# Diagonals in two column halves, a first block of its own, re-dealt PSUM banks and earlier transposed loads in a fused forward and backward kernel

## The chip, the cores and the metric

The kernel runs on one core of a Trainium2 chip. A core has a matrix engine (TensorE, PE in the profile, with its weight loads as PEld), a vector engine (VectorE, DVE), a scalar engine (ScalarE, ACT), GpSimd (POOL) and a sync engine (SyncE, SP) that here only issues DMAs. All engines run their own instruction streams in order and meet at semaphores. The metric is the device time of one execution in microseconds; a kernel's time is the median of several executions.

## The reference

The function computes a layer, and then the gradients of all its inputs for a given `grad_out`. S is 2048 rows, D is 1024, F is 3584, all bf16:

```python
xn = layernorm(A_q)
# branch A: short convolution of k, times v, then a long convolution along S by FFT
kv = (sum over t of k shifted by t, times shift_k) * v
y  = irfft(rfft(pad(kv)) * rfft(pad(ssm_k)))[:S] + kv * ssm_D
s  = xn * y
# branch B: gated product of two projections and a third one back
h  = (xn @ w_gate) * (xn @ w_up)
g  = silu(h @ w_down)
out = A_q + s * g
```

The outputs are `out` and the gradients by `A_q` (called dx), k, v, `shift_k`, `ssm_k`, `ssm_D`, `w_gate`, `w_up` and `w_down`. Two of them are sums over S for each channel alone: the gradient of `ssm_D` is the sum of dy times kv, and that of `shift_k` is, for each of four shifts, the sum of dk times the shifted k. The kernel computes such a sum as the diagonal of a 128x128 matrix product.

## The kernel before, in words

The 2048 rows are 16 blocks of 128, the 1024 channels 8 slices of 128, and the 3584 hidden columns 14 slabs of 256. U0 to U12 are SBUF regions of 8 KB a partition that change their use from stage to stage. The stages follow each other on PE:

1. **Layer norm and the first two slabs** (to about 60 us). `layer_norm` (L495 and on) takes the blocks in chunks of 2, 2, 4, 4 and 4 and writes transposed, normalised blocks (PE transposes at L542); `gu_unit` multiplies a chunk with a slab of both projections (L567), copies it to `gut` (ACT, L569), multiplies the two halves on DVE to `hN`, and puts off the transposes of `hN` (`turn`, L581) with `defer`. `flush(age)` raises the age of all that is put off and runs those that have reached it; `gu_unit` calls it after every block. `hN` and `gut` have two buffers each.
2. **The other slabs, with the forward convolution** (to 586 us). `make_pump` runs the convolution's generator alongside: each `yield` gives a weight, meant as the step's DVE time in us, and `pump` advances until the weights done reach the share of the matmul units done.
3. **h @ w_down and the gate** (to 796 us). L964 makes two PSUM banks for a block; `gate` turns them on ACT and DVE into `out` and the gradients that the rest needs, `dbm` among them, and defers its transposes (L1003).
4. **dh and the gradients of w_gate and w_up** (796 to 1451 us). `dh_half` (L1082) and `dw_slab` (L1101) share the PSUM tiles `psb`, which ACT copies out (L1084 to `dht`, L1105 to `wb`); DVE multiplies `dht` into the `U` tiles. The backward convolution runs alongside through `bpump`: first `dy_forward` (per slice: the diagonal product at L803 for the gradient of `ssm_D`, then a forward transform through `psS` and `psP`), then 16 units of `product`, `inv8` and a tail, whose matmuls (L407, L904) write the PSUM tile `psY` that ACT copies out (L882, L906).
5. **The gradient of w_down** (1451 to 1690 us, L1181), into `psb` too. Its outputs leave from U12 by DMAs on SP's queue. SP also issues here the transposing loads of w_gate and w_up (`load_wgu`, L1152) for the next stage.
6. **dx** (1690 us to the end): `dx_part` (L1212) multiplies transposed pieces of the gradient (`dgut`, read by transposing DMAs at L1206 on SP's queue) with those weights, 14 pieces for each group of four blocks; `ln_backward` ends each block. `dk_units` runs alongside, with the diagonal product at L939: for each slice and half, 8 weight loads of 128 columns and 8 matmuls of 512 columns, which are four shifts of 128.

In stages 4 and 5 the eight PSUM banks are dealt out as 4 for `psb`, 1 each for `psS` and `psP`, and 2 for `psY`.

The order of the instructions on each engine is made by a planner: it takes them by priority (the program's order, unless `high_priority` or `issue_after` says otherwise) as their inputs and buffers come free in its own reckoning, so that an engine can be given later work early. On the chip each engine then keeps that order.

Of the kernel before, what the change touches and what calls it, by code (L numbers as in the profile page):

```python
# [19 lines left out]
def build_kernel(  # L20
# [98 lines left out]
    warm = const.tile([P, 1], F32, name="warm")  # L119
    nc.vector.memset(warm[:], 1.0)  # L120
    nc.scalar.activation(warm[:], warm[:], ACT.Sqrt)
    RSTD = const.tile([P, NB], F32, name="RSTD")
    Dbc = const.tile([P, D], BF16, name="Dbc")
    Wbc = const.tile([P, 4, D], BF16, name="Wbc")
# [73 lines left out]
    def tt(o, a, b, op):  # L198
        V.tensor_tensor(o, a, b, op)  # L199
# [101 lines left out]
    def product(A, B, O, wp, conj, src, parts=2):  # L301

        n = 8 // parts
        dst = 1 - src
        for q in range(parts):
            sl = slice(q * n, (q + 1) * n)
            a, b, o = cv(A[:])[:, sl], cv(B[:])[:, sl], cv(O[:])[:, sl]
            m = wp.tile([P, 3, n, 2, 256], BF16, name="m", tag="W")
            m1 = m[:, 0].rearrange("p f k (c d) -> p f k c d", c=2)
            m2 = m[:, 1].rearrange("p f k (c d) -> p f k c d", c=2)  # L310
            n1 = m[:, 2].rearrange("p f k x -> p (f k x)")[:, 0:n * 256].rearrange("p (f k d) -> p f k d", f=n, k=2)
            n2 = m[:, 2].rearrange("p f k x -> p (f k x)")[:, n * 256:].rearrange("p (f k d) -> p f k d", f=n, k=2)
            fk = "p f k c d -> p (f k) c d"
            tt(m1.rearrange(fk), a.rearrange(fk), b.rearrange(fk)[:, :, 0:1, :].to_broadcast([P, 2 * n, 2, P]), MUL)
            for k in range(2):
                tt(m2[:, :, k], a[:, :, k], b[:, :, 1 - k, 0:1, :].to_broadcast([P, n, 2, P]), MUL)
            yield 2.8
            b1, asrc = b[:, :, :, 1, :], a[:, :, :, src, :]
            tt(n1, asrc, b1, MUL)
            tt(n2, asrc, b1[:, :, ::-1], MUL)  # L320
            tt(m1[:, :, :, dst], m1[:, :, :, dst], n1, ADD)
            tt(m2[:, :, :, dst], m2[:, :, :, dst], n2, ADD)
            yield 2.8
            tt(o[:, :, 0], m1[:, :, 0], m1[:, :, 1], ADD if conj else SUB)
            if conj:
                tt(o[:, :, 1], m2[:, :, 1], m2[:, :, 0], SUB)
            else:
                tt(o[:, :, 1], m2[:, :, 0], m2[:, :, 1], ADD)
            yield 1.4
    PROD_W = 14.0  # L330

    def turned(X, to, frm, sign):
# [226 lines left out]
    def gu_unit(sl, b0, n, w, tick):  # L559

        gut = fg.tile([P, 4, 2, SLW], BF16, name="gut")
        hN = fg.tile([P, 4, SLW], BF16, name="hN")
        for i in range(n):
            q, qi = divmod(b0 + i, 4)
            ps = ps_gu.tile([P, 512], F32, name="psg")
            for dc in range(DC):
                gu_mm[0] = nc.tensor.matmul(ps[:], XNT[q][:, dc, qi * P:(qi + 1) * P],  # L567
                                            w[:, dc].rearrange("p a f -> p (a f)"), start=(dc == 0), stop=(dc == DC - 1))
            nc.scalar.copy(out=gut[:, i].rearrange("p a f -> p (a f)"), in_=ps[:])  # L569
            flush(2)  # L570
            tick()
        sta(GUd[sl, b0 // 8][:, b0 % 8:b0 % 8 + n], gut[:, 0:n])
        tt(hN[:, 0:n], gut[:, 0:n, 0], gut[:, 0:n, 1], MUL)
        st(Hd[sl][:, b0:b0 + n, :], hN[:, 0:n])

        def turn():
            hT = fg.tile([P, 2, 4, P], BF16, name="hT")
            ps = ps_tr.tile([P, 2, 4, P], BF16, name="tr")
            for a in range(2):
                for i in range(n):  # L580
                    nc.tensor.transpose(ps[:, a, i, :], hN[:, i, a * P:(a + 1) * P], ident[:])  # L581
            nc.scalar.copy(out=hT[:, :, 0:n], in_=ps[:, :, 0:n])
            fr, so = sl % 12 * SLW, b0 % 8 * P
            st(HTd[b0 // 8][sl // 12][fr:fr + SLW, so:so + n * P].rearrange("(a f) s -> f a s", f=P),
               hT[:, :, 0:n].rearrange("f a i s -> f a (i s)"))
        defer(turn)

    def conv_forward():
# [90 lines left out]
        for ds in range(8):  # L679
# [7 lines left out]

    F_TOTAL = 4 * 20.0 + 8 * (0.2 + FWD4_W + FWD2_W + 1.4 + 1.2 + PROD_W + INV_W + 1.6)
    nop = lambda: None
    slabs = [load_slab(0, nc.scalar)[0]]  # L690
    chunks = [(0, 2), (2, 2), (4, 4), (8, 4), (12, 4)]
    xs = [(b0, n, u8((4, 6, 7)[b0 // 4 - 1], a=4) if n == 4 else lnp.tile([P, n, D], BF16, name=f"x{b0}")[:])
          for (b0, n) in chunks]
    for c in xs[:2]:
        ln_load(*c)
    slabs.append(load_slab(1, nc.sync)[0])
    for c in xs[2:]:
        ln_load(*c)

    def copy_k(dp):  # L700
# [8 lines left out]
    for i, (b0, n, x4) in enumerate(xs):  # L709
# [2 lines left out]
                last, root, xst = layer_norm(*xs[i + 1])  # L712
        for sl in range(2):
            gu_unit(sl, b0, n, slabs[sl], nop)
            if i in (2, 3):
                with tc.issue_after(gu_mm[0].ins):
                    for j in ((3, 4), (2,), (1,), (0,))[2 * (i - 2) + sl]:
                        bcast(j)
        if i == len(xs) - 1:
            with tc.issue_after(root.ins):  # L720
# [67 lines left out]
    def dy_forward(cx, cs):  # L788
# [7 lines left out]
        for ds in range(8):  # L796
# [3 lines left out]
            X = cs.tile([P, 16, 256], BF16, name="DX")  # L800
            ps = ps_y.tile([P, 4, P], F32, name="psY")
            for b in range(NB):
                nc.tensor.matmul(ps[:, 0, :], x[:, b, :], kv[:, b, :], start=(b == 0), stop=(b == NB - 1))  # L803
            yield 0.1
            dt_ = cs.tile([P, P], F32, name="dt_")
            tt(dt_[:], ps[:, 0, :], ident_f[:], MUL)
            dr_ = cs.tile([P, 1], F32, name="dr_")
            V.tensor_reduce(dr_[:], dt_[:], AX.X, ADD)
            V.tensor_copy(ddo[:, ds:ds + 1], dr_[:])
# [5 lines left out]
    def conv_backward():  # L815
        cx = pool("d_cx", 2)
        cs = pool("d_cs", 1)
        yield from dy_forward(cx, cs)
        cs.release()
        cx.release()  # L820
        tfp.release()
# [55 lines left out]
    def dkv_tail(ds, G, tiles, ew):  # L877
        dy, v, ksh = tiles
        y = ew.tile([P, NB, P], BF16, name="yl")
        for rp in range(4):  # L880
            ps = inv8_rows(G, ps_y, rp)
            nc.scalar.copy(out=by_res(y[:], rp), in_=rowps(ps))  # L882
            yield 0.1
        tt(dy[:], dy[:], Dbc[:, ds * P:(ds + 1) * P].unsqueeze(1).to_broadcast([P, NB, P]), MUL)
# [10 lines left out]
    def dh_tail(ds, G, ew):  # L895
        hr = ew.tile([P, 2, 8, P], BF16, name="yl")
        ho = ew.tile([P, 2, P, 8], BF16, name="ho")
        for c in range(2):
            for rq in range(2):
                ps = ps_y.tile([P, 4, P], F32, name="psY")  # L900
                for i in range(4):
                    r = 4 * rq + i
                    for k in range(2):
# [8 lines left out]
    def dk_units(ew, psp):  # L912
# [11 lines left out]
        for i in range(16):  # L924
# [9 lines left out]
                yield 1  # L934
            st(o_dk[:, c, :, dsl], acc[:])
            if c == 0:
                ps = psp.tile([P, 4, P], F32, name="psdk")
            for r in range(8):
                nc.tensor.matmul(ps[:].rearrange("p a b -> p (a b)"), dk[:, r, :],  # L939
                                 kh[:, r:r + 4, :].rearrange("p a b -> p (a b)"),  # L940
                                 start=(c == 0 and r == 0), stop=(c == 1 and r == 7))
            yield 1
            if i < 15:
                kh, dk = load(i + 1)
            if c == 1:
                dt_ = ew.tile([P, 4, P], F32, name="dt2")
                tt(dt_[:], ps[:], ident_f[:].unsqueeze(1).to_broadcast([P, 4, P]), MUL)
                dr_ = ew.tile([P, 4], F32, name="dr2")
                V.tensor_reduce(dr_[:], dt_[:], AX.X, ADD)
                V.tensor_copy(dsko[:, ds, ::-1], dr_[:])  # L950
# [105 lines left out]
    XN = [u8(q, a=4) for q in (7, 8, 9, 10)]  # L1056
    bg = pool("bg", 2, side="right")
    U.append(bg.tile([P, 4096], BF16, name="U12", bufs=1))
    ps_b = ps_tr = pool("ps_b", 4, space=PSUM)
    tr_name[0] = "psb"  # L1060
    ps_c3 = pool("ps_c3", 1, space=PSUM)
    ps_y = pool("ps_y3", 2, space=PSUM)
    bcnt = [0]
    BT = NSL * (8 + 16) + 84.0

# [48 lines left out]
        ld(h, Hd[sl])  # L1114
        return h

    flush()
    for k in (1, 2):
        gu_in(k)
    wdts = [wdt, load_wdt(1)]  # L1120
# [3 lines left out]
        gu_in(k)  # L1124
    first = dh_half(0, wdt)
    DBM = [u8(q, a=4) for q in (0, 1, 4, 5)]
    HSL = (3, 11, 6, 2)
    for sl in range(NSL):
        dgus = [first, dh_half(2 * sl + 1, wdts[sl])]
        if sl + 2 < NSL:  # L1130
# [10 lines left out]
        for k in (2 * sl + 5, 2 * sl + 6):  # L1141
            gu_in(k)

    pieces = [(a, j) for j in range(7) for a in range(2)]
# [2 lines left out]
    def load_wgu(n, store):  # L1149
        a, j = pieces[n]  # L1150
        WGU[n] = store
        nc.sync.dma_start_transpose(out=store, in_=(B_w_gate, B_w_up)[a][:, j * 512:(j + 1) * 512])  # L1152

    flush()
    for k in range(NSL):
        if 0 < k and k + 1 < NSL:
            hs[k + 1] = load_h(k + 1, HSL[(k + 1) % 4])
        if k == 0:
            hs[2] = load_h(2, HSL[2])
        if k in (1, 3, 5, 7):  # L1160
            load_wgu(k // 2, u8(7 + k // 2, a=4))
        if k == 11:

            bdrain()
# [1 line left out]
            gw = pool("gw", 1)  # L1166
            gd = pool("gd", 1)
            for i in range(2):
                load_wgu(4 + i, gw.tile([P, 4, D], BF16, name=f"W{i}")[:])
            load_wgu(6, u8(6, a=4))  # L1170
        if k == 12:
            load_wgu(7, u8(2, a=4))
        if k == 13:
            load_wgu(8, u8(3, a=4))
        h = hs.pop(k)
        for f in range(2):
            wbs = U[12][:].rearrange("p (i d) -> p i d", i=4)[:, (2 * k + f) % 4]
            for dh in range(2):
                ps = ps_b.tile([P, 512], F32, name="psb")
                for b in range(NB):  # L1180
# [3 lines left out]
                btick(2)  # L1184
            f0 = k * SLW + f * P
            ld(o_dwd[f0:f0 + P, :], wbs)
    for p_ in (ps_y, ps_c3, ps_b, bg, bw):
        p_.release()

    gd2 = pool("gd2", 1, side="right")
    gl = pool("gl", 2, side="right")
    gs = pool("gs", 4, side="right")
    kw_ = pool("kw", 1)
# [1 line left out]
    ps_k = pool("ps_k", 1, space=PSUM)  # L1198
    kpump, kdrain = make_pump(dk_units(kw_, ps_k), DK_TOTAL)
    kcnt = [0]  # L1200

    def load_dgut(g, n):

        a, j = pieces[n]
        t = (gd, gd2)[n // 7].tile([P, 4, 512], BF16, name=f"dgut{n}")
        nc.sync.dma_start_transpose(out=t[:], in_=DGd[j, a, 512 * g:512 * g + 512, :])  # L1206
        return t

    def dx_part(t, i, ps, n, dhs=(0, 1)):
        for f in range(4):  # L1210
# [34 lines left out]
            V.scalar_tensor_tensor(dx_t[:, cl], dxn[:, cl], RSTD[:, b:b + 1], dout_t[:, cl], op0=MUL, op1=ADD)  # L1245
            (st if parts == 1 else ld)(o_dx[:, c, r, cl], dx_t[:, cl])

    ts = [load_dgut(0, n) for n in range(7)]
    for i, j in enumerate((11, 0, 1, 4, 5)):
        load_wgu(9 + i, u8(j, a=4))  # L1250
        ts.append(load_dgut(0, 7 + i))
    ts += [load_dgut(0, n) for n in (12, 13)]
    for g in range(4):
        for b in (4 * g, 4 * g + 2):
            if b == NB - 2:
# [86 lines left out]
```

## Time and profile before

| | us |
|---|---|
| time, median of 4 runs (2087.7 to 2102.53) | 2095.59 |
| time of the profiled execution | 2091.74 |
| its span, first to last instruction | 2089.9 |
| PE busy | 2005.5 (96%) |
| DVE busy | 1461.2 (70%) |
| ACT busy | 626.6 (30%) |
| granted TensorE clock, mean | 0.99 |

A row of the waits reads: engine, tile and line of the instruction that waited, then what released it, and then the total in us, the number of waits and the longest. A row of the stretches reads: from and to, length, and the busy time of each engine with its number of instructions, the granted clock, the mean share of the DMA engines and GB/s. A row of the timeline reads: start, duration, engine, line, operation, tiles, number, and in brackets the idle time before it and what ended that.

### The profile page before, as it was taken

What the parts mean: (1) busy time and instruction counts of PE and PEld (TensorE: products, weight loads), DVE (VectorE), ACT (ScalarE), POOL (GpSimd) and SP (SyncE); (2) the same over time, 40 slices, a digit from 0 to 9 for tenths busy, and PEclk for the clock granted to TensorE, in tenths of its full rate; (3) what the DMA queues carried; (4) which work ended last, traced back from release to release, by engine and by line L of the source; (5) the groups of instructions that cost most, each with busy time, mean ns of one, the idle gap of its engine ahead of it and who ended that gap; (6) DMA issues with size and microseconds to landing.
All of it is one profiled execution on the core that took longest, in us unless ns stands there. A gap on an engine that the chain in (4) does not pass through costs nothing.

```text
span 2089.9 us, 28857 instructions
## 1 busy us (share of the span) xinstructions
PE 2005.5 (96%) x11438; PEld 1089.2 (52%) x11626; DVE 1461.2 (70%) x1937; ACT 626.6 (30%) x969; POOL 340.5 (16%) x496
## 2 busy tenths in 40 slices
PE   7989999999999998999899999999999989999998
PEld 3455555555544446666566555564444434444443
DVE  7689898878725555787799999899596024344443
ACT  5734444444423333222222222222122101111112
POOL 3322222121112121000112112111111000110100
PEclk9999999999999999999999999999999999999999
DMA  8776677566598878666889978767964989393921
GB/s 291 239 254 207 219 234 251 185 215 241 174 313 266 258 239 311 217 210 155 264 250 266 228 229 276 217 222 219 228 220 137 230 196 226 94 210 92 222 72 58
DMA packets 454279, 451.29 MB, mean 216 GB/s; under 512 B 236944, under 2 KB 380600, under 8 KB 439680
## 3 DMA queue, kind: packets, MB, share of 16 engines
q1 hardware_dynamic: 308096, 185.89, 34.6%
q0 software_dynamic: 45120, 189.08, 26.9%
q10 hardware_dynamic: 100928, 74.47, 11.6%
q8 instruction: 91, 1.49, 0.3%
q14 instruction: 44, 0.36, 0.1%
HBM read 208.15 MB, written 194.02 MB: 192 GB/s over the span
## 4 chain that ended last, share of the span: by engine, by line
PE 42%; DVE 6%; issue 6%; SPq 4%; DMA 3%; POOL 1%; ACT 0%; another core or an unknown queue 0%; ACTq 0%; DVEq 0%; POOLq 0%
PE psx L1212 17%; PE psb L1101 11%; PE psb L1181 7%; PE psb L1082 4%; SPq L1152 3%; DVE W L199 2%; DVE m L199 1%; PE psdk L939 1%; DVE U L199 1%; DMA dyl<-DYd 1%; DMA B<-HFd 1%; PE psY L904 0%; PE psY L407 0%; SPq L1206 0%; DMA U<-GUd 0%
## 5 line engine op out<-in xcount | busy, mean ns | idle before, releaser
L1101 PE MATMUL psb<-U,U 128*128 128x512 bf16 x1746 | 402.2, 384 | 10.5 <-ACT dht L1084 4.7
L567 PE MATMUL psg<-wslab,U 128*128 128x512 bf16 x1729 | 403.3, 381 | 4.2 <-ACT gut L569 0.7
L1212 PE MATMUL psx<-U,dgut 128*128 128x512 bf16 x1508 | 336.3, 380 | 7.1 <-DMA dgut<-DGd 5.4
L1212 PEld LDWEIGHTS <-dgut 128*128 128x128 bf16 x1792 | 175.6, 98 | 219.0 <-DMA dgut<-DGd 6.9
L1101 PEld LDWEIGHTS <-U 128*128 128x128 bf16 x1792 | 176.9, 99 | 212.3 <-issue 19.3
L567 PEld LDWEIGHTS <-U 128*128 128x128 bf16 x1792 | 173.6, 98 | 187.9 <-issue 5.5
L1082 PE MATMUL psb<-wdt,U 128*128 128x256 bf16 x1792 | 205.9, 275 | 0.0
L569 ACT CAST gut<-psg 128x512 bf16<-128x512 f32 x224 | 131.1, 586 | 219.5 <-PE psg L567 216.7
L1181 PE MATMUL psb<-U,U 128*128 128x512 bf16 x875 | 195.8, 380 | 1.1
L1082 PEld LDWEIGHTS <-U 128*128 128x128 bf16 x1792 | 176.5, 99 | 23.2
L964 PE MATMUL psbm<-U,ht 128*128 128x512 bf16 x766 | 170.4, 379 | 1.2 <-DMA ht<-HTd 0.3
L1105 ACT CAST wb<-psb 128x512 bf16<-128x512 f32 x112 | 65.7, 586 | 320.4 <-PE psb L1101 252.2
L199 DVE TENSOR_TENSOR W<-W 128x1024 f32<-128x1024 f32 (+1 forms) x144 | 149.7, 1058 | 2.7
L199 DVE TENSOR_TENSOR m<-A,B 128x1024 bf16<-128x1024 bf16 (+1 forms) x160 | 116.7, 792 | 40.5 <-issue 22.3
L1181 PEld LDWEIGHTS <-U 128*128 128x128 bf16 x896 | 87.4, 98 | 102.7 <-issue 1.3
L1235 ACT ACTIVATE dx_t<-dxn 128x1024 bf16<-128x1024 f32 (+1 forms) x17 | 17.1, 1007 | 361.8 <-DVE dxn L199 309.8
L199 DVE TENSOR_TENSOR dka<-dkh,Wbc 128x1024 bf16<-128x1024 bf16 x16 | 11.1, 692 | 160.4 <-DMA dkh<-DKSHd 160.4
L964 PEld LDWEIGHTS <-ht 128*128 128x128 bf16 x784 | 76.0, 98 | 89.5 <-DMA ht<-HTd 0.8
L1084 ACT CAST dht<-psb 128x512 bf16<-128x512 f32 x112 | 65.1, 588 | 149.2 <-PE psb L1082 99.3
L1183 ACT CAST U<-psb 128x512 bf16<-128x512 f32 x56 | 32.8, 587 | 164.2 <-PE psb L1181 126.2
L199 DVE TENSOR_TENSOR U<-U,dht 128x2048 bf16<-128x2048 bf16 x56 | 68.1, 1220 | 19.0 <-ACT dht L1084 19.0
L199 DVE TENSOR_TENSOR gg<-bm,sig 128x1024 bf16<-128x1024 bf16 x16 | 11.1, 692 | 91.9 <-ACT sig L982 91.9
(239 smaller groups left out, 2471.4 us busy)
## 6 DMA issues: line engine op xcount, KB each, us to landing
U<-GUd SPq DMA_DIRECT2D x28, 1024.0 KB, 7.0
DGd<-U ACTq DMA_DIRECT2D x56, 512.0 KB, 5.7
GUd<-gut ACTq DMA_DIRECT2D x54, 512.0 KB, 4.5
A<-DYFd POOLq DMA_DIRECT2D x16, 1024.0 KB, 6.4
U<-Hd SPq DMA_DIRECT2D x15, 1024.0 KB, 6.7
out_dram<-wb ACTq DMA_DIRECT2D x224, 64.0 KB, 3.2
Hd<-hN POOLq DMA_DIRECT2D x54, 256.0 KB, 4.6
HTd<-hT POOLq DMA_DIRECT2D x54, 256.0 KB, 4.1
```

The costliest lines, as they stand in the source:

```text
L199: V.tensor_tensor(o, a, b, op)
L567: gu_mm[0] = nc.tensor.matmul(ps[:], XNT[q][:, dc, qi * P:(qi + 1) * P], w[:, dc].rearrange("p a f -> p (a f)"), start=(dc == 0), stop=(dc ...
L569: nc.scalar.copy(out=gut[:, i].rearrange("p a f -> p (a f)"), in_=ps[:])
L964: nc.tensor.matmul(ps[:, dh * 512:(dh + 1) * 512], ht(fc)[:, i * P:(i + 1) * P], WD[fc // 4][:, fc % 4, dh * 512:(dh + 1) * 512], start=(f ...
L1082: nc.tensor.matmul(ps[:, x * SLW:(x + 1) * SLW], DBMT[2 * hf + g][:, dc, (b % 4) * P:(b % 4 + 1) * P], wdt[:, dc, :], start=(dc == 0), sto ...
L1084: nc.scalar.copy(out=dht[:, 2 * e:2 * e + 2].rearrange("p b f -> p (b f)"), in_=ps[:])
L1101: nc.tensor.matmul(ps[:], XN[b // 4][:, b % 4, dc * P:(dc + 1) * P], dgus[b // 8][:, b % 8].rearrange("p a f -> p (a f)"), start=(b == 0), ...
L1105: nc.scalar.copy(out=wb[:].rearrange("p a f -> p (a f)"), in_=ps[:])
L1152: nc.sync.dma_start_transpose(out=store, in_=(B_w_gate, B_w_up)[a][:, j * 512:(j + 1) * 512])
L1181: nc.tensor.matmul(ps[:], h[:, b, f * P:(f + 1) * P], DBM[b // 4][:, b % 4, dh * 512:(dh + 1) * 512], start=(b == 0), stop=(b == NB - 1))
L1183: nc.scalar.copy(out=wbs[:, dh * 512:(dh + 1) * 512], in_=ps[:])
L1212: nc.tensor.matmul(ps[:, dh * 512:(dh + 1) * 512], t[n][:, f, i * P:(i + 1) * P], WGU[n][:, f, dh * 512:(dh + 1) * 512], start=(n == 0 and ...
```

## The change

- **Diagonals.** The product at L803 is made as two products of 64x64, one for each half of the channels, which write the partitions 0 to 63 and 64 to 127 of one PSUM tile; that at L939 as two of 64 x (4 x 64). The mask is a new 128x64 constant `diag`, both halves of the identity in one. DVE's masked multiply and sum take half the columns.
- **First chunk.** The chunks are 1, 1, 2, 4, 4, 4 blocks. The load of the first block comes ahead of slab 0, which moves from ACT's queue to SP's. The places where the broadcast rows are made move on by one chunk.
- **Pace.** The weights that `product` yields become 5.6, 5.6 and 2.8 divided by the number of parts.
- **`flush(3)`** instead of `flush(2)` in `gu_unit`. At the end of stage 3, what is put off gets age -2 instead of being run at once.
- **PSUM.** `psb` gets 3 banks, `psS` and `psP` 2 each, `psY` 1; when `dy_forward` is through, the four of `psS` and `psP` become four `psY` tiles for the tails.
- **Stage 5.** Its outputs leave from a pool `wo` of four tiles, h has three homes instead of four, w_gate and w_up pieces are loaded at steps 1, 2, 3, 4, 5 (before: 1, 3, 5, 7), and the `dgut` pieces of group 0 at steps 6 to 9, 11, 12 and 13 and after; before, all of them after the loop.

```diff
+    diag = const.tile([P, 64], F32, name="diag")
+    nc.vector.tensor_tensor(diag[:], ident_f[:, 0:64], ident_f[:, 64:128], ADD)
...
-            yield 2.8
+            yield 5.6 / parts
...
-            yield 1.4
+            yield 2.8 / parts
...
-            flush(2)
+            flush(3)
...
-    slabs = [load_slab(0, nc.scalar)[0]]
-    chunks = [(0, 2), (2, 2), (4, 4), (8, 4), (12, 4)]
+    chunks = [(0, 1), (1, 1), (2, 2), (4, 4), (8, 4), (12, 4)]
...
-    for c in xs[:2]:
+    ln_load(*xs[0])
+    slabs = [load_slab(0, nc.sync)[0]]
+    for c in xs[1:3]:
...
-                nc.tensor.matmul(ps[:, 0, :], x[:, b, :], kv[:, b, :], start=(b == 0), stop=(b == NB - 1))
+                for j in (slice(0, 64), slice(64, 128)):
+                    nc.tensor.matmul(ps[j, 0, 0:64], x[:, b, j], kv[:, b, j], start=(b == 0), stop=(b == NB - 1))
...
         yield from dy_forward(cx, cs)
+        ps_c3.release()
+        ps_y4.append(pool("ps_y4", 4, space=PSUM))
...
-                nc.tensor.matmul(ps[:].rearrange("p a b -> p (a b)"), dk[:, r, :],
-                                 kh[:, r:r + 4, :].rearrange("p a b -> p (a b)"),
-                                 start=(c == 0 and r == 0), stop=(c == 1 and r == 7))
+                for j in (slice(0, 64), slice(64, 128)):
+                    nc.tensor.matmul(ps[j], dk[:, r, j], kh[:, r:r + 4, j],
+                                     start=(c == 0 and r == 0), stop=(c == 1 and r == 7))
...
-    ps_b = ps_tr = pool("ps_b", 4, space=PSUM)
+    ps_b = ps_tr = pool("ps_b", 3, space=PSUM)
...
-    ps_c3 = pool("ps_c3", 1, space=PSUM)
-    ps_y = pool("ps_y3", 2, space=PSUM)
+    ps_y = pool("ps_y3", 1, space=PSUM)
+    ps_c3 = pool("ps_c3", 2, space=PSUM)
...
-    flush()
+    for e in later:
+        e[0] = -2
...
-        if k in (1, 3, 5, 7):
-            load_wgu(k // 2, u8(7 + k // 2, a=4))
+        if k in (1, 2, 3, 4, 5):
+            load_wgu(k - 1, u8((7, 8, 9, 10, 2)[k - 1], a=4))
+        if k in (6, 7, 8, 9):
+            ts.append(load_dgut(0, k - 6))
...
-    ts = [load_dgut(0, n) for n in range(7)]
     for i, j in enumerate((11, 0, 1, 4, 5)):
         load_wgu(9 + i, u8(j, a=4))
-        ts.append(load_dgut(0, 7 + i))
-    ts += [load_dgut(0, n) for n in (12, 13)]
+        ts.append(load_dgut(0, 9 + i))
```

## The prediction, made before the result was known

> **What bounds the kernel now.** I read the page's busy times first, then the stretches of each stage, then what PE waited for.
>
> ```profile
> PE 2005.5 (96%) x11438; PEld 1089.2 (52%) x11626; DVE 1461.2 (70%) x1937; ACT 626.6 (30%) x969; POOL 340.5 (16%) x496
> ...
> 796.00:1000.00 204.00, 202.76 (x1374) 130.54 (x1389) 156.44 (x236) 58.78 (x103) 14.35 (x27) 0.99 0.71 213
> 1000.00:1451.00 451.00, 431.47 (x2652) 260.30 (x2683) 422.28 (x488) 111.47 (x198) 83.38 (x114) 0.98 0.80 242
> ...
> 1706.00:2081.00 375.00, 372.94 (x1701) 169.66 (x1734) 155.17 (x200) 54.54 (x79) 36.58 (x58) 1.00 0.60 140
> ```
>
> PE is the bound: it idles 84 us of 2090, and in the stretches where the diagonals lie (796 to 1000, 1706 to 2081) it idles 1.2 and 2.1 us. What PE saves or spends there counts in full. From 1000 to 1451 DVE is busy 94% too, so there PE's waits are DVE's lateness, handed on by ACT. PE's own waits are the rest that can be won:
>
> ```profile
> PE tr L542 <- DVE x L539: 11.0, 1, 11.0
> PE tr L581 <- DVE hN L199: 8.9, 10, 2.6
> PE psb L1003 <- DVE dbm L199: 6.7, 1, 6.7
> PE psx L1212 <- DMA dgut<-DGd: 5.4, 3, 3.1
> PE psb L1101 <- ACT dht L1084: 4.7, 2, 4.4
> PE psY L407 <- ACT yl L882: 4.4, 2, 3.8
> ...
> PE psY L904 <- ACT yl L906: 2.8, 1, 2.8
> PE psY L407 <- DVE B L242: 2.8, 1, 2.8
> ```
>
> Nearly every wait in this list is addressed by an edit, so I price the edits against it.
>
> **Pace weights: 0.** `product` has two parts by default and both callers leave it so: 5.6/2 and 2.8/2 are the old 2.8 and 1.4. This edit does nothing.
>
> **`flush(3)`: -6.6 us.** It puts the transposes of `hN` one block, 8 matmuls (8 x 0.216 = 1.7 us), later. Of the 8.9 us of waits, one of 1.4 us at 585.8 is the last unit, which the final `flush()` still runs at once; the longest, 2.6, leaves 0.8; the rest fits into 1.7. 8.9 - 1.4 - 0.8 = 6.7, say 6.6. The ACT copy and POOL store of `hT` come 1.7 us later; their readers are a stage away. Range -4 to -7.
>
> **Age -2 at the end of stage 3: -5.5 us.** PE now starts `dh_half(0)`, which needs only the first eight blocks, and the transposes follow after its four `psb` (7 us). The wait of 6.7 us goes. What comes late next: ACT's copy of the last `psbm` (1.0 us, ended 1.2 us after PE's last matmul), which I take as the new first wait if the first `psb` lies in its banks. DVE's gate ends at 797.1; the `dht` copies have two buffers and its first multiplication is then due, so little queues behind. Range -3 to -6.7.
>
> **First chunk: -1.5 us.** PE begins at 11.0 because DVE does two blocks first, from 5.5. One block saves two statistics pairs and scalings, about 1.6 us of the 5.5, and its 256 KB, alone in front, may land in 3.1 to 4.9 us (the rows of such loads) after its issue at 0.74 where the first data came at 5.5. Against this: slab 0 leaves ACT's queue for SP's and is issued about 0.5 us later (0.45 us an issue), so the later loads, slab 1 among them, stand behind two more issues; a chunk more costs DVE another chain of small operations, about 2 us from 8.3 to 10.5; and units of one block reuse two `gut` buffers after 1.7 us of work where the store lands after 4.5 to 5.8 us. Range -3.5 to +2.
>
> **Gradient pieces: -5.4 us.** Rows of the profile's transposing loads:
>
> ```profile
> L1206 SPq DMA_TRANSPOSE dgut<-DGd x56: 1809/2302/6182, 1631.4 to 1980.7; - x56
> L1152 SPq DMA_TRANSPOSE U<-in_B_w_gate_dram x6: 4419/5676/24397, 1449.1 to 1689.1; - x6
> ```
>
> From 1610 to 1708 SP issues ten weight and fourteen gradient loads, 90 us of issuing in 98 us, and PE meets three pieces not yet there. One weight load (5.7) and four pieces (4 x 2.3) leave this stretch for earlier steps, where SP mostly waits for ACT: it ends some 15 us sooner, the waits go. The nine pieces pass the remaining outputs, h and the row loads in SP's queue; an output held up by 2.3 us leaves from four tiles, used again 28 us later, so it is covered. Not covered is a burst: at 1473 one weight load held SP for 24.4 us, ACT waited 18.1 us for outputs, and PE 2.8. A fifth weight load sits near that place. h with three homes is still loaded a step ahead. Range -6 to +3.
>
> **PSUM: +3.9 us.** A trace row shows the case where `psb` counts:
>
> ```profile
> 1153.23 0.59 ACT L1084 CAST dht<-psb 128x512 bf16<-128x512 f32 x1 [10.15 <-DVE U L199]
> ```
>
> ACT waits for DVE with four `psb` full, PE stops for 4.4 us. I compared each `psb` group's first weight load with the end of ACT's copy three groups earlier. With three banks seven places run short: at 1027 by 0.6, 1120 by 0.7, 1147 by 6.4 (1.75 more than now), 1198 by 3.9, 1293 by 2.3 (0.5 of it there now), 1347 by 0.4, 1380 by 1.85. The one at 1198 takes the place of the 3.8 us that PE waits for `yl` at 1207, in the same ACT stall: net 0.1. Sum 0.6 + 0.7 + 1.75 + 0.1 + 1.8 + 0.4 + 1.85 = 7.2. Four `psY` remove the other `yl` waits, 0.6 and 2.8: +3.8 to 3.9. The waits for `B` stay, they are DVE's. Two banks each for `psS` and `psP`: 0, since PE hardly idles there. Range -3 (if the spare `psY` let PE run ahead in every stall) to +12.
>
> **Diagonals: -6 us.** The rows of before are these:
>
> ```profile
> L803 PEld LDWEIGHTS <-dyx x128: 97/98/98, 814.8 to 973.4; 128*128 128x128 bf16 x128
> L803 PE MATMUL psY<-kvx,dyx x128: 219/219/219, 814.9 to 973.5; 128*128 128x128 bf16 x128
> ...
> L939 PE MATMUL psdk<-kh,dkh x124: 379/379/379, 1658.4 to 2023.4; 128*128 128x512 bf16 x124
> ...
> 1730.13 1.73 PE psdk L939 x8
> ```
>
> Eight dk matmuls take 1.73 us, 0.216 each, 16 times: 27.7 us. If the two column halves run side by side a pair takes as long as one matmul of 256, 0.109 (L1082 makes sixteen in 1.75): 14.0 us, so -13.8. If they run one after the other, 2 x 0.109: +0.3. The dy product is 16 matmuls in about 0.9 us (0.056 each), 8 times: 7.2 us. Halves of 64 columns have little to win there: side by side 0, with each half taking the time of a whole one +7.2.
>
> [...] I take dk at -9 and dy at +3, near the middle, as neither end has a row behind it. Range -14 to +15. DVE's halved mask work is not on PE's path at either place.
>
> **Sum.** -6.6 - 5.5 - 1.5 - 5.4 + 3.9 - 6 = -21.1. The profiled execution, 2091.7 (span 2089.9 and 1.8 around it), becomes 2070.6. It ran 3.9 under the median, so the same step from the median 2095.6 gives **2074.5**. The last 9 us, after PE's last matmul, are unchanged. The likeliest case's own range is 2060 to 2085. About 0.5% (10.5 us: under 2085.1 or over 2106.1) is what a measurement can tell from no change.
>
> **Rivals.**
>
> [...]
>
> *PSUM and SP's queue take back more.* Three `psb` cost 11 with no gain from `psY`, and the burst of weight loads eats 3.4 of the 5.4. -6.6 - 5.5 - 1.5 - 2 + 11 - 6 = -10.6, **2085**. For it: 94% DVE from 1000 to 1451, four stalls of ACT of 4 to 10 us. Against: most stalls are shorter than three groups (5.2 to 10.4 us).
>
> [...]
>
> **Chances.** Main case 0.58, nearly all of it faster; no overlap 0.18 (0.03 faster, 0.11 same, 0.04 slower); banks and queue 0.14 (0.06, 0.06, 0.02); exposed loads 0.10 (slower by 0.09). Faster 0.66, same 0.19, slower 0.15. The range reaches from the main case with every part at a good value (-40: start 3.5, `hN` 7, turn 6.7, pieces 6, diagonals 14, PSUM 3) to just past the second case: **2055 to 2100**, which leaves out the exposed loads and half of what is over 2096.
>
> **What would show it.** `hN` waits of PE near 1 to 2 us; no `dbm` wait at 796; no `dgut` waits after 1690; PE's first matmul before 10 us; `psdk` groups of 1.2 us or less where 1.73 stood, and `psY` groups at L803 of 0.9 to 1.6; waits of `psb` on ACT risen from 4.7 to about 12 and those of `yl` gone. I am wrong if the `psdk` groups stay at 1.7 or grow, if ACT's stalls stop PE for over 15 us, or if outputs held up behind SP's transposing loads stop ACT in stage 5.

## The result and the profile after

The changed kernel takes 2084.37 us (median of 44 runs, 2073.82 to 2100.82); the kernel before took 2093.81 (63 runs). The ratio of the two, each time taken beside the other's, is 0.9963, with a 95% interval of 0.9950 to 0.9976: 7.8 us less (5 to 10.5). 2074.5 and 21 us less were predicted, so the sign was right, the time lies in the stated range, and the gain is little more than a third of the forecast.

The profiled execution was one of the quicker ones (2079.1 us, span 2077.3). Its busy times, stretches cut at its own stage borders, and PE's waits:

```profile
PE 1986.1 (96%) x11691; PEld 1086.4 (52%) x11882; DVE 1450.9 (70%) x1949; ACT 625.1 (30%) x972; POOL 342.4 (16%) x501
...
794.00:1000.00 206.00, 196.44 (x1480) 125.40 (x1493) 156.44 (x239) 60.20 (x104) 15.64 (x28) 0.99 0.77 221
1000.00:1458.00 458.00, 434.35 (x2679) 263.55 (x2709) 423.16 (x492) 112.55 (x199) 83.78 (x114) 0.98 0.77 240
...
1706.00:2068.00 362.00, 356.65 (x1783) 165.62 (x1816) 149.26 (x197) 54.53 (x79) 35.36 (x56) 1.00 0.63 142
```

```profile
PE tr L583 <- DVE hN L201: 10.6, 6, 8.5
PE psb L1089 <- ACT dht L1091: 9.1, 2, 6.0
PE tr L544 <- DVE x L541: 8.0, 1, 8.0
PE psY L420 <- DVE HX L201: 5.9, 4, 2.1
PE psY L807 <- DMA kvx<-KVd: 4.6, 1, 4.6
PE psg L569 <- ACT U L545: 4.5, 2, 3.5
PE psY L409 <- DVE B L244: 4.5, 1, 4.5
...
PE psb L1108 <- ACT dht L1091: 2.9, 2, 1.6
```

PE is busy 19 us less, and it still idles 91 us of the span. The list has no `dbm` of 6.7 us, no `dgut` and no `yl` any more, as foretold; but `hN` stands at 10.6 where it was to fall to 1 to 2, and waits for `kvx` and for ACT's `U` are new. The `dht` row of 9.1 is not: 6.0 of it stand at 1157.8, in the stall that cost 4.4 at 1153.9 before, and 3.1 at 1297.6, near another place that the prediction named. The stretch from 794 to 1000 went from 1.2 us of idle PE to 9.6.

Where the time went is seen best between fixed points of PE's program, which have the same work between them in both kernels but for the diagonals and a few matmuls at two of the borders (starts of weight loads: the one after the n-th of the projections, the first of each stage; dw is the gradients of w_gate and w_up; us):

| stretch | before | after | difference | predicted |
|---|---|---|---|---|
| start to 320th load of the projections | 104.6 | 109.3 | +4.7 | -1.5 |
| 320th to 1280th load | 324.4 | 319.1 | -5.3 | |
| 1280th load to stage 3 | 157.2 | 163.8 | +6.6 | with the line above -6.6 |
| stage 3 to the first dw load | 236.2 | 236.5 | +0.3 | -5.5 |
| first dw load to stage 5 | 628.9 | 629.4 | +0.5 | about +10 (`psb` +7.2, `yl` -0.6, dy +3) |
| stage 5 (to the first load of dx) | 207.8 | 203.3 | -4.5 | -2.8 (`yl`) |
| dx, first to last load | 421.1 | 406.0 | -15.1 | -14.4 |
| last load to the end | 9.7 | 10.1 | +0.4 | 0 |

The sum is -12.4, the span's -12.6 within the rounding. Stage 5 and dx earn more than all of it. The gains on `hN`, at the start and at the end of stage 3 are absent or have turned round: 13.6 us were forecast for the three, and 6.3 were lost.

### The profile page after: what moved, and what is told of

Same layout as the page of the kernel before. It is cut to its first block, busy times and chain, and to the rows that moved or that the text cites. A ratio compares the mean times of both kernels' runs of the same rounds, so it can differ in the third digit from the quotient of the medians.

```text
span 2077.3 us, 29391 instructions
## 1 busy us (share of the span) xinstructions
PE 1986.1 (96%) x11691; PEld 1086.4 (52%) x11882; DVE 1450.9 (70%) x1949; ACT 625.1 (30%) x972; POOL 342.4 (16%) x501
## 4 chain that ended last, share of the span: by engine, by line
PE 51%; issue 23%; DVE 15%; POOL 4%; DMA 4%; ACT 1%; ACTq 0%; POOLq 0%; SPq 0%; DVEq 0%
PE psx L1229 18%; PE psb L1108 10%; PE psb L1206 9%; PE psg L569 5%; PE psb L1089 4%; DVE m L201 4%; DVE W L201 3%; DVE HX L201 2%; DVE U L201 2%; DVE KX L201 1%; DMA dyl<-DYd 1%; PE psP L218 1%; PE psdk L946 1%; PE psS L218 1%; POOL HTd L65 1%
## 5 line engine op out<-in xcount | busy, mean ns | idle before, releaser
L1108 PE MATMUL psb<-U,U 128*128 128x512 bf16 x1746 | 397.3, 382 | 8.6 <-ACT dht L1091 2.9
L1108 PEld LDWEIGHTS <-U 128*128 128x128 bf16 x1792 | 176.0, 98 | 210.6 <-issue 12.2
L1089 PE MATMUL psb<-wdt,U 128*128 128x256 bf16 x1792 | 206.0, 275 | 10.3 <-ACT dht L1091 9.1
L1206 PE MATMUL psb<-U,U 128*128 128x512 bf16 x875 | 194.7, 379 | 1.1
L201 DVE TENSOR_TENSOR W<-W 128x1024 f32<-128x1024 f32 (+1 forms) x144 | 142.7, 1009 | 2.7
L1208 ACT CAST wbs<-psb 128x512 bf16<-128x512 f32 x56 | 32.8, 585 | 159.6 <-PE psb L1206 135.5
```

Source lines behind the costliest of these rows:

```text
L1089: nc.tensor.matmul(ps[:, x * SLW:(x + 1) * SLW], DBMT[2 * hf + g][:, dc, (b % 4) * P:(b % 4 + 1) * P], wdt[:, dc, :], start=(dc == 0), sto ...
L1108: nc.tensor.matmul(ps[:], XN[b // 4][:, b % 4, dc * P:(dc + 1) * P], dgus[b // 8][:, b % 8].rearrange("p a f -> p (a f)"), start=(b == 0), ...
L1206: nc.tensor.matmul(ps[:], h[:, b, f * P:(f + 1) * P], DBM[b // 4][:, b % 4, dh * 512:(dh + 1) * 512], start=(b == 0), stop=(b == NB - 1))
L1208: nc.scalar.copy(out=wbs[:, dh * 512:(dh + 1) * 512], in_=ps[:])
```

## The experiments

The number after "Measured" is the ratio to the kernel before, which ran beside each; the changed kernel's is 0.9963. The median of the kernel before was 2094.3 us beside the first four, 2089.2 beside the next four and 2097.4 beside the last three, so medians in us should not be compared from one of these groups to another. Single executions of one kernel scatter by 12 to 30 us, so the intervals are 5 to 8 us to either side, and where an effect is smaller the stretches of the profiled executions are read instead. Where nothing moved, most of these repeat within 3 us from kernel to kernel; the one from the first dw load to stage 5 lies between 624.9 and 629.4 in the ten kernels that have neither late loads nor a later pump there. Stage 5 and a place near 1010 us scatter more, and are taken up below.

**The diagonals alone**, in the kernel before: the edits at L803 and L939 and the constant `diag`.

> The kernel before with the two diagonals in column halves (and the mask `diag`) and nothing else. Theory 1, the halves run side by side and each edit's gain can be lost again only next to where it is made: PE's groups go from 1.73 to about 1.1 us (dk, 16 times) and from 0.9 to 0.7 (dy, 8 times), the time falls by 11 to 12 us, the stretch from the first to the last matmul of dx shortens by about 10. Theory 2, the planner's new order decides and an edit's place says little: the groups shorten likewise, but the time falls by less than 6 us or rises, with new waits far from the diagonals.

Measured: 0.9952 (0.9923 to 0.9982), 10 us less, with an interval that holds both -4 and -16. The groups settle it. These are pieces of the chain of waits, first of this kernel, then, for the dy product, of the changed one:

```profile
1744.86 2.38 PE psx L1215 x11
1747.24 0.99 PE psdk L943 x16
1748.23 3.35 PE psx L1215 x15
```

```profile
839.98 2.75 PE psb L1108 x12
842.74 0.62 PE psY L807 x32
843.36 0.33 PE psS L218 x2
```

Sixteen matmuls of 256 columns start to start in 0.99 us where eight of 512 took 1.73; within a group the two halves start 2 to 4 ns apart and the next pair 0.109 us later, the turn of one matmul of 256: the halves run side by side. At either end of a group a tenth is lost: the matmul ahead of it keeps the group waiting for 0.309 where 0.216 is its turn, and the last pair takes 0.205 for 0.109. With both ends a dk group costs 1.73 - 0.99 - 0.09 = 0.64 us less, 16 times 10.2 us; a dy group 0.89 - 0.63 - 0.09 = 0.17, 8 times 1.4. Together 11.6 us, as theory 1 has it for the groups. Its other sign, dx shorter by 10 us, did not show in this profiled execution (a span of 2104.2): dx took 423.2 us for 421.1, as PE waited 8.0 for `dgut` and 4.3 for `dxn`, and stage 5 took 11.4 longer, which comes under the paced loads. In the changed kernel, where the `dgut` waits are gone too, dx is 15 us shorter.

**The old start** in the changed kernel: chunks 2, 2, 4, 4, 4 and slab 0 on ACT's queue.

```diff
-    chunks = [(0, 1), (1, 1), (2, 2), (4, 4), (8, 4), (12, 4)]
+    slabs = [load_slab(0, nc.scalar)[0]]
+    chunks = [(0, 2), (2, 2), (4, 4), (8, 4), (12, 4)]
...
```

> The changed kernel with the chunks 2, 2, 4, 4, 4 and slab 0 on ACT's queue, as before. Theory 1, a first block of its own costs time, because ACT's copy of its transposes stands behind the next block's root and because units of one block wait for the stores of `gut`: the 320th weight load of the projections comes at about 105 us again instead of 109.3, and the time is 4 to 5 us under the changed kernel's. Theory 2, the late 320th load comes from the later transposes (`flush(3)`) or from DMA order: it stays at 108 or later and the time is the same within 2 us.

Measured: the 320th load came at 104.2 us, 5.1 sooner than in the changed kernel, as theory 1 has it, though PE there begins at 11.0 instead of 8.0. The 320th load came at 104 to 105 us in all seven kernels with the old chunks, and at 109 in the six others. The time as a whole, 0.9967 (0.9945 to 0.9990), doesn't show it; the profiled execution has an unrelated wait of 5 us for h in stage 5. The changed kernel's timeline shows the first reason, ACT's order:

```profile
11.39 0.20 ACT L520 ACTIVATE r__233<-vpe 128x1 f32<-128x1 bf16 x1 [5.14 <-DVE vpe L518]
11.50 0.99 ACT L545 COPY U<-tr 128x1024 bf16<-128x1024 bf16 x1
```

The transposes of block 0 are ready at 9.1. But the planner put the root of block 1 ahead of their copy on ACT, and that root waits for DVE, which does block 1's statistics and, between them, the new `diag` (1.3 us at 9.54). PE waits 3.5 us; later ACT waits twice 3.3 us for `gut` tiles still being stored, and PE 1.0 and 2.1 for ACT. How the loss divides between these was not tried.

**The gate's last transposes at once**, as before, in the changed kernel.

```diff
-    for e in later:
-        e[0] = -2
+    flush()
```

> The changed kernel with the last transposes of the gate run at once at the end of stage 3, as before. Theory 1, the wait saved there comes back as PE's wait for `kvx` and `dyx`, since the chain from the gate to the first dy product is as long as before: the wait for `dbm` of about 6.7 us returns, the 4.6 us wait for `kvx` goes, and the time is the changed kernel's within 2 us. Theory 2, the wait for `kvx` has another cause (the new PSUM deal, POOL's queue): it stays and the time is 6 to 7 us over the changed kernel's.

Measured: 0.9952 (0.9926 to 0.9978), the profile 2076.9 beside the changed kernel's 2077.3. Of PE's waits

```profile
PE psb L1089 <- ACT dht L1091: 9.5, 2, 6.4
PE tr L544 <- DVE x L541: 7.8, 1, 7.8
PE psb L1009 <- DVE dbm L201: 6.7, 1, 6.7
```

the 6.7 us are back, and the wait for `kvx` is gone. From stage 3 to the first dw load it takes 235.3 us, with the edit 236.5. Theory 1: the edit is worth nothing. The first dy product needs the last block's `dy` written to memory and read back (gate, `DYd`, `dyx`), and the load of `kvx`, which itself needs nothing of the gate, stands behind that of `dyx` on POOL's queue. From the last matmul of stage 3 to the landing of `kvx` it takes 21.3 us before, 22.4 in the changed kernel and 21.6 here, whatever PE does meanwhile. Issuing `kvx` ahead of `dyx` was not tried; `dyx` landed 1.5 us sooner than `kvx`, and it is needed too.

The trace shows too what the wait of 6.7 us costs beside its length. After it, stretches of the kernel before read

```profile
796.00:800.00 4.00, 4.00 (x24) 3.08 (x25) 1.15 (x2) 1.01 (x1) 1.19 (x3) 0.50 1.02 420
804.00:812.00 8.00, 8.00 (x76) 7.18 (x74) 3.19 (x3) 2.67 (x5) 1.05 (x2) 1.00 1.02 402
```

The granted clock is 0.50 in the first, and dh's matmuls start 0.213 us apart there where 0.109 is their turn. So without the wait PE comes to the dy product 18.1 us after the last weight load of stage 3 where it took 26.3: 8.2 us sooner, 5.5 of them the wait. All of it is lost again: 4.6 us in the wait for `kvx`, 3.0 at `psS` and `psP` for ACT and DVE, which the pause seems to have held up too, and about 1 in slow matmuls after that wait (a clock of 0.57 from 816.4 to 820).

**The old PSUM deal** in the changed kernel (`psb` 4, `psS` and `psP` 1, `psY` 2, no `ps_y4`).

> The changed kernel with the PSUM banks dealt as before: 4 for `psb`, 1 each for `psS` and `psP`, 2 for `psY` to the end. Theory 1, three `psb` lengthen what PE loses when ACT waits for DVE: PE's waits of `psb` on ACT fall from 12 to about 5 us, those of `psY` on `yl` return with 3 to 7 us, and the time is 2 to 6 us under the changed kernel's. Theory 2, the spare `psY` are worth more than the bank of `psb`: the time is 2 us or more above it.

Measured: 0.9962 (0.9934 to 0.9990); from the first dw load to stage 5 627.0 us, with the new deal 629.4. PE's waits of `psb` on ACT are 5.2 where they were 12.0, those on `yl` 4.4 where there were none: both as theory 1 says, but they nearly cancel, and 2.4 us is within what this stretch scatters between kernels with the new deal (624.9 to 629.4). From stage 3's first load to stage 5 it is 865.2 us for 865.7. The deal is worth nothing that can be measured here, and neither theory's time came.

**`flush(2)`** in the changed kernel.

> The changed kernel with `flush(2)` in `gu_unit`, as before. Theory 1, putting the transposes off made the planner set DVE's first product of the gate (`so`, which waits for a load) ahead of the last `hN`: with `flush(2)` the order is `hN`, `so` again, the wait of 8.5 us at the end of stage 2 falls to about 1.4, the stretch from the 1280th weight load of the projections to stage 3 to 157 us from 163.8; and the waits for `hN` during the convolution come back with about 5 us between the 320th and the 640th load (110 to 111 us for 105), so that the time is within 2 us of the changed kernel's. Theory 2, the 8.5 us come from elsewhere: they stay, and the time is 5 us above.

Measured: 0.9968 (0.9941 to 0.9996). From the 1280th load to stage 3 157.2 us for 163.8, from the 320th to the 640th 110.8 for 105.0: theory 1 in both halves. Putting the transposes off wins 5.3 us between the 320th and the 1280th load, where DVE is late with `hN` (over all the profiled kernels 319.1 to 322.0 us with `flush(3)`, 323.6 to 324.4 with `flush(2)`), and 6.6 are lost at the end, where the last `flush()` runs the transposes at once in either kernel. That loss is one swap in DVE's order, in the changed kernel (first ACT's copy that makes the last `gut`):

```profile
583.02 0.59 ACT L571 CAST gut<-psg 128x512 bf16<-128x512 f32 x1 [0.67 <-PE psg L569]
...
590.13 0.69 DVE L201 TENSOR_TENSOR so<-xn_t,yf_t 128x1024 bf16<-128x1024 bf16 x1 [13.16 <-DMA yf_t<-YFd]
590.74 0.69 DVE L201 TENSOR_TENSOR hN<-gut 128x1024 bf16<-128x1024 bf16 x1
```

`gut` was ready at 583.6, but `so` stands first and waits for a load until 590.1. In the kernel before `hN` stands first, and PE waited 1.4 us there.

**The last `hN` ahead of `so`** in the changed kernel, the only difference in DVE's order:

```diff
-        tt(hN[:, 0:n], gut[:, 0:n, 0], gut[:, 0:n, 1], MUL)
+        hn_last[0] = V.tensor_tensor(hN[:, 0:n], gut[:, 0:n, 0], gut[:, 0:n, 1], MUL)
...
-        tt(so, xn_t, yf_t, MUL)
+        with tc.issue_after(hn_last[0].ins):
+            tt(so, xn_t, yf_t, MUL)
```

> The changed kernel with one swap: DVE's last `hN` ahead of the gate's first product `so`; nothing else in DVE's order differs. Theory 1: the wait of 8.5 us at the end of stage 2 falls to 1 to 2, stage 3 starts 6 to 7 us sooner and the time falls by 5 to 7 us. Theory 2, the wait moves on: PE then waits in stage 3 for the loads of w_down, ht or the gate, and the time stays within 2 us.

Measured: 0.9937 (0.9911 to 0.9963), 2076.97 us. The stretch to stage 3 is 156.3 us, 7.5 less; the wait is 1.4; stage 3 takes 203.3 to its end for 201.8, a wait of 1.8 for w_down. So some 6 us stay won in the profile, theory 1; the ratio falls by about 5 us, though its interval still meets the changed kernel's.

**The transposing loads of stage 5 paced**, each behind its step's load of h:

```diff
-        if k in (1, 2, 3, 4, 5):
-            load_wgu(k - 1, u8((7, 8, 9, 10, 2)[k - 1], a=4))
+        with tc.issue_after(h_ld[0].ins):
+            if k in (1, 2, 3, 4, 5):
+                load_wgu(k - 1, u8((7, 8, 9, 10, 2)[k - 1], a=4))
...
```

(the four `dgut` loads at 6 to 9 likewise.)

> The changed kernel with the transposing loads of stage 5 held behind the same step's load of h in SP's queue, so that one goes out each step instead of nine in the first 60 us. Theory 1, the burst is why some executions lose 5 to 12 us in stage 5 (PE waits for h behind a transposing load that takes 20 us), which the profiled execution of the changed kernel was spared: the median falls by 3 to 5 us and the stretch from stage 5's first to stage 6's first weight load stays at 203 us or less. Theory 2, the losses are not the burst's: the median stays within 2 us, or the pieces come too late and PE waits for `dgut` again.

Measured: 0.9939 (0.9912 to 0.9966), 2078.77 us; stage 5 stays at 203.3. By the ratio that is 5 us under the changed kernel, but the two intervals overlap, and against the kernel before beside each the medians differ by 1 us (10.4 and 9.4 less): the time alone doesn't show theory 1. The profiles speak for it. In all five kernels with paced loads stage 5 took 203.3 us; of the six others with the new stage 5, three took 203.3 and three 210.6 to 221.1, 6.5 more than 203.3 on average. These are single executions. What the burst does is plain where it struck, in the kernel with the old banks. First SP's queue there, then PE's longest wait:

```profile
1480.99 21.75 SPq L1162 DMA_TRANSPOSE U<-in_B_w_up_dram  x1
1502.83 0.53 SPq L62 DMA_DIRECT2D out_dram<-wbs  x1
1503.46 10.61 SPq L1162 DMA_TRANSPOSE U<-in_B_w_gate_dram  x1
1514.12 5.57 SPq L1168 DMA_TRANSPOSE dgut<-DGd  x2
1519.79 0.53 SPq L62 DMA_DIRECT2D U<-Hd  x1
```

```profile
PE psb L1203 <- DMA U<-Hd: 11.9, 1, 11.9
```

The planner does not spread the loads over the steps where the program has them: it sets all nine within 60 us, and between one load of h and the next up to four of them. If each is issued in 6 to 10 us, as in the changed kernel's profiled execution, h comes in time; if one holds SP for 22, PE stops for 12. With the loads paced, one held SP for 14.8 us, and PE lost nothing. The stage took 210.6 us with the old start, 217.3 with the old banks, 221.1 with `flush(2)`, and 219.2 with the diagonals alone, where the burst has four weight loads and no pieces; one of these held SP for 33.0 us. The kernel before has that burst as well, with this load in its profiled execution:

```profile
1473.09 24.40 SPq L1152 DMA_TRANSPOSE U<-in_B_w_gate_dram  x1
```

ACT then waits 18.1 us for output tiles and PE 2.8 for ACT.

**Four mends together**: old start, the swap, the paced loads, and the convolution's pump started 4 ticks later, so that 48 more matmuls of dh stand before the first dy product.

```diff
-        bpump((bcnt[0] - 8) / (BT - 8))
+        bpump((bcnt[0] - 12) / (BT - 12))
```

> The changed kernel with four mends: the old chunks and slab order, the last `hN` ahead of `so`, the paced loads, and the backward convolution's pump starting 4 ticks later, so that 48 more matmuls of dh (5.2 us) stand before the first dy product. Theory 1, the losses are local and add up: -5 (start), -7 (`hN`), -5 to -8 (`kvx` and what follows) in the profile, about -17 us, and some 3 more in the median by the pacing: about 2065. Theory 2, the planner's new order loses as much elsewhere: the time is within 6 us of the changed kernel's.

Measured: 0.9892 (0.9854 to 0.9931), 2068.40 us: by the ratio 15 us under the changed kernel, in the profile 12.7. That is nearer to theory 1, which had 17 for the profile, than to theory 2. The pump, though, did not do its part: the wait for `kvx` is gone, but a wait for `psS` of 6.0 us and others took its place, and from stage 4's first load to the end of the fourth slab of dw it took 224.5 us where the changed kernel takes 218.7.

**Three mends**, without the later pump.

> The mended kernel without the later pump start, so three mends: old chunks and slab order, the last `hN` ahead of `so`, the paced loads. Theory 1, the later pump only moved the loss: the wait for `kvx` (4 to 6 us) returns, but the stretch from stage 4's first load to the fourth slab of dw (224.5 us in the mended kernel) falls to 216 to 219, and the time to about 2062. Theory 2, the later pump was worth its 4.6 us: the time rises to 2073 or more.

Measured: 0.9897 (0.9865 to 0.9929). The stretch named is 218.9 us and the `kvx` wait 4.7, as theory 1 has it; but by the ratio the time is the same, as neither theory has it. (The median, 2076.84, would be theory 2's, but the kernel before ran 8 us longer beside it than beside the four mends.) The profiled execution was a long one (a span of 2086.8), with a single stop of 15.2 us near 1034. DVE and ACT just before it:

```profile
1026.55 3.63 DVE L201 TENSOR_TENSOR m<-A,B 128x2048 bf16<-128x2048 bf16 x5 [26.49 <-DMA B<-HFd]
```

```profile
1008.79 24.17 ACTq L68 DMA_DIRECT2D out_dram<-wb  x2
```

The first product of the backward convolution waits for its loads, and ACT itself hangs 24 us in issuing two stores of `wb`, so `psb` isn't emptied. One thing sets this kernel and the last one below apart from the others: when a transposing load (`wdt`, w_down for stage 4) was issued. With it, in all thirteen profiled kernels, how long `A` and `B`, the loads of that first product, took to land (us):

| kernel | `wdt` issued, against the store of `DYFd` | first `A` | first `B` |
|---|---|---|---|
| the ten others | 0.8 to 3.4 us after it | 7.7 to 9.6 | 10.0 to 11.9 |
| four mends | 3.0 us ahead of it | 7.9 | 10.3 |
| three mends | 0.4 us ahead | 25.3 | 27.3 |
| three mends, turn at once | 0.7 us ahead | 18.8 | 20.9 |

ACT's issuing goes the same way: the longest single issue on its queue there (985 to 1045 us) took 13.4 to 13.7 us in the three kernels with `wdt` ahead, and 5.9 to 9.6 in the ten others. That they go together is seen; that the one causes the other was not tried.

**The three mends with four `psb` and, later, four `psY`** (`psY` two until `dy_forward` is through).

> The three mends with `psb` back at four banks, `psS` and `psP` at one each, `psY` at two until `dy_forward` is through and then at four, made of the banks of both. Theory 1, the lost bank of `psb` costs PE 4 to 7 us between 1000 and 1451 us, so the stretch from the first dw load to stage 5 (about 629 us) falls by 4 to 7 and the time likewise. Theory 2, ACT's stalls behind DVE are longer than a bank more can cover: the stretch stays within 2 us.

Measured: 0.9912 (0.9878 to 0.9946), not apart from the three mends. From the first dw load to stage 5 627.5 us, 1.9 under the changed kernel's: theory 2 by its own bound. The direct comparison, with this stretch in the three mends, is spoiled by the stop of 15 us there, and this kernel has a wait of its own of 4.3 us for `wdt` at 1151.8, at the place of one of ACT's stalls. What the four and four would win without these stays open.

**The three mends with the turn at once.**

> The three mends with the gate's last transposes run at once, as before. Theory 1, the moved transposes are worth nothing, as PE waits for the first dy product's data instead: from stage 3's first load to the first dw load it takes within 2 us of the same with them moved. Theory 2, the two waits only met by chance of timing: it takes 4 us or more longer, and the time rises by as much.

Measured: 0.9911 (0.9879 to 0.9944). From stage 3's first load to the first dw load 236.2 us, with the transposes moved 238.2: theory 1 again, at the edge of its 2 us.

## Why the prediction was right and wrong

What failed is that three waits, and what lay behind them, were taken as time that can be won: `hN`, the start and `dbm`. -13.6 us were forecast for the three, and +6.3 measured, because the planner set DVE's order anew, because ACT's copy stood behind a later block's root, and because another product's data were due just behind the third. That the time still fell inside the range is in part luck: the diagonals brought 5.6 us more than forecast. The 2085 us of the rival on PSUM and SP's queue is met by the number alone; its reason, `psb` at +11, did not come.

**Right:** PE as the bound; the pace weights as no edit at all; the pieces (no `dgut` wait is left, in each kernel that has them); dx as a whole, -15.1 for -14.4, though in other parts: the dk diagonals -10.2 for -9, the pieces -5.4, and a new wait for `dxn` of +2.4. Neither of the cases on the halves came, no overlap or exposed loads: the halves start 2 to 4 ns apart, and their weight loads are covered, at 0.109 us a pair.

**Diagonals, -6: too small by half.** The term that was mis-sized is above all dy's, +3 for a measured -1.4; dk's was -9 for -10.2. Each was a choice between halves that run side by side (-13.8 and 0) and dearer ones, and no run shows the losses that put dk at -9 and dy at +3: they were my estimate. In their place the runs showed 0.09 and 0.10 us lost at the ends of a group, and weight loads that keep up: half-width loads come in pairs within 0.109 us in dk, and in dy thirty-two matmuls start within 0.50 us, a pair every 32 ns. The measured term is -11.6.

**`flush(3)`, -6.6: it gave +1.3.** The step "of the 8.9 us, one of 1.4 is the last unit" treated the edit as a shift of waits that were in the trace. The waits it shifts did go (-5.3). But with the transposes moved the planner also gave DVE a gate operation ahead of the last `hN`; by what reckoning was not looked into. The swap alone, undone, brought 6 us.

**First chunk, -1.5: it gave +4.7**, outside its range. I had both causes in hand, a chunk more of small operations and the two `gut` buffers against their stores, but set them at 2 us in all against PE's earlier beginning. PE began 3 us sooner and then stood: the copy on ACT behind a root that waits was not in the sum, nor was the mask's 1.3 us on DVE. With the old chunks the mask costs nothing (the 320th load at 104 to 105 us with and without it); here it lies on that root's way.

**Age -2, -5.5: +0.3.** I asked what was late next on ACT and DVE, and found the 1.15 us for `bm` as they came. I didn't ask what PE meets 20 us later: a product whose data come by way of memory, timed from the gate. The wait was only moved to it. Nor did I see that the wait cost more than its 6.7 us, as PE ran at half the clock (0.50) behind it.

**PSUM, +3.9:** +0.5 to +2 by the old deal, which can't be told from nothing. PE's waits of `psb` on ACT are 12.0 us, as foretold, but at other places in part: of the seven, those at 1147, 1198 and 1293 came, with 6.0, 1.4 and 3.1 us, and the one at 1027 with 0.4; those at 1120, 1347 and 1380 did not, and one of 1.6 at 1252 was not among them. The `yl` wait of 2.8 us, which I gave to the spare `psY`, belongs to the burst in stage 5: ACT was late with `yl` because it waited for output tiles. With the old deal in the changed kernel it did not come back.

**The burst** was named as "not covered" and put into the range, but not into the sum. The profiled execution of the changed kernel was spared it. It may be why the profiles differ by 12.6 us and the times by 8 to 9, but pacing didn't change the time by more than the intervals leave open. What share the kernel before pays for its own smaller burst was not tried.

With the measured terms the sum is +4.7 + 1.3 + 0.3 + 2 - 11.6 - 5.4 - 2.8 = -11.5 for the profiled execution, where -12.6 was measured. The rest of stage 5's line, and of dx's beside the new wait of 2.4 us for `dxn`, is an us or two each and stays unexplained.

## What to carry to other kernels

A wait in the list is worth its time only if nothing else is due just after it: for each, follow PE's program on to the next operand that comes through memory, and time that chain from where it really starts. Look also at the granted clock behind a long wait (0.50 here after 6.7 us): slow matmuls there are part of its price. Where a planner sets each engine's order, an edit moves the order on the others as well, so look at the neighbours of the moved instruction on every engine, and pin the one that matters. And take loads that hold a queue for 10 to 20 us (here 10.6, 14.8 and 21.8 us) as events that will sometimes coincide: what they are put ahead of must have that much time to spare.

## What the runs showed that I had not expected

- Thirty-two matmuls of 64 columns on two column halves start within 0.50 us, two at a time and a pair every 32 ns, and their weight loads keep up. The whole-width product that they replace takes 56 ns a matmul. Entering and leaving such a group costs about 0.1 us each.
- After a wait of 6.7 us the granted clock was 0.50, and the next 24 matmuls of dh started 0.213 us apart instead of 0.109, some 2.5 us more; after the wait of 1.15 us at 795.5 they kept to 0.109.
- A transposing load issued 0.4 to 0.7 us ahead of other queues' transfers goes with landings of 19 to 27 us where 8 to 12 is usual, and with a stop of 18 and 24 us in which ACT issues two stores; issued after them it goes with no such landings and itself takes 23 to 26 us to land, and issued 3 us ahead it takes 5. That is read from thirteen executions, two of them with the late landings; it was not tried by moving the load alone, and what the transfers contend for stays open.
- Where DVE's instruction behind another's late load is ready long before, nothing is gained by its being short: 0.7 us of `hN` cost PE a wait of 8.5.
